# The last two value products of a block move beside the next block's first scores, and the attention steps are spread evenly

## Chip, core and metric

The kernel runs on one core of one Trainium2 chip. The metric is the device time of one execution in microseconds. Three executions of the kernel before took 840.87, 840.63 and 839.79 us, so the median is 840.63 us.

## What is computed

Windowed attention over 8 batches, 8 heads, 576 positions and head dimension 64, and then a feed-forward layer on the 4608 resulting tokens of width 512:

```
scores = q @ k^T / 8, kept where 0 <= row - col < 64
attn   = softmax(scores);  x = attn @ v, heads side by side: 4608 x 512
h = x @ w_in                               (512 x 2048)
g = h where h >= 1, 0 where h <= -1, else (h + 1)^2 / 4
out = g @ w_out                            (2048 x 512)
```

Products of full float32 precision are made of three matmuls each (high by high, high by low, low by high), so every operand is split into a rounded high part and a low rest.

## The kernel before

**Tiles and blocks.** The tokens are cut into nine tiles of 512. The first three (t = 0, 1, 2; `PLAIN = 3`) go through the feed-forward layer chunk by chunk: 16 chunks f, each an in-projection (`ffn_in`, L1153, 12 matmuls into one bank of the PSUM pool `ps_h`), a gate on ScalarE, VectorE and GpSimd (`add_gate`: relu L1163, square L1168, gate L1175, high part L1180, low part L1185), and an out-projection (`ffn_out`, L1199, 12 matmuls into four banks `acc`). The other six tiles are handled in pairs as three blocks (`SUPERS = 3`): sums of weight quarters and of token quarters replace one product in eight, so a block is 56 products into `ps_h` and `acc` (`ffn_product`, L928; I write P) and 56 out of it into `acc` (`out_product`, L1014; O), 6 matmuls each. The weight sums are made while tiles 1 and 2 run (`add_sums`: L842, L849, L857 on VectorE or GpSimd, a copy on ScalarE, a store to `kept` in DRAM), in two buffers, so a half of a sum waits until the store of the half before the last has landed.

**Attention steps.** A step s covers 128 tokens, four to a tile. Its scores (S, `att_scores`, L439) go to two banks `ps_a`; VectorE masks them and takes the maximum (L462, eight instructions and as many reads), ScalarE takes the exponentials (L482), VectorE or GpSimd normalizes (L501), VectorE transposes (L508), and the result goes through DRAM (`moved`, then `ptd`). After that the values (V, `att_values`, L552) can be multiplied. Steps 0 to 11 belong to the three tiles, 12 to 19, 20 to 27 and 28 to 35 to the three blocks; a block takes its steps in the order 0, 4, 1, 5, 2, 6, 3, 7. When the values of a token quarter's two steps are there, VectorE, ScalarE and GpSimd build the token sums and their high and low parts (`add_build`: L587, L290, L623).

**Pairs.** From step 9 on TensorE takes the scores of one step and the values of an earlier one as one piece, without a break (`do` in `add_step`). The values of tile 2's last step and of the last two steps of each block (`BEHIND = 2`) are pieces of their own, and so are the scores of steps 12 and 16, and of the first two steps of the later blocks. A value product alone takes a bank of `ps_a`; a paired one takes a bank of `ps_h` or of `acc` (the name `pj` in `add_step`). `ps_a` and `ps_h` have two banks each, `acc` has four.

**Order.** `Plan` sets the order on every engine in advance: each piece of work has a key (its due time), a cost and its dependences, and each engine takes the piece that could start first, by key among those about equal. Keys of attention steps come from `a_keys`: backwards from the block's start with a lead and a distance (`A_SUPER`), in units of about four microseconds. The instructions then run in that order, engine by engine, whatever the chip's times turn out to be.

Of the kernel before, what the change touches and what calls it, by code (L numbers as in the profile page):

```python
# [22 lines left out]
SB = 2 * QB  # L23
# [5 lines left out]
TILES = [512] * 9  # L29
# [11 lines left out]
JOIN = 8  # L41
BEHIND = 2
E_SPAN = 0.29
E_LEAD = 9.81
W_LEAD = -1.5
W_FIRST = (17.22, -2.0, 1.41, 1.48, -3.05)
W_STEP = 1.02
L_LEAD = -0.77
W_LATE = (3.72, -1.06, -2.67, 7.19, 13.28, 13.03, 18.55)
# [6 lines left out]
M_LATE = 1  # L56
W0_STEP = 12.29
FINE = 4
# [5 lines left out]
A_LEAD = 4.64  # L64
O_LAG = 2.79
O_LAG_DMA = 2300
# [11 lines left out]
B_PE = 2210  # L78
B_DUE = (2.44, -1.28, -0.74)
B_STEP = 5.68  # L80
B_FIRST = 1.45
A_END = 5.86
V_PE = 1270
NORM = dict(Pool=800, DVE=480), dict(DVE=610)
G_LATE = (1.94, 1.65, -4.21, -4.45, 2.08)
D_LATE = (-0.7, 0.46, 6.3, -3.34, 6.37, 0.12)
# [11 lines left out]
SUM_KEEP = 1150  # L98
V_LATE_2 = 14.69
PATIENCE = dict(ACT=300, DVE=0, Pool=303, PE=0, SP=0)  # L100
# [5 lines left out]
SUPERS = 3  # L106
H_STEP = 18.67
S_LATE = 1.62
S_PACE = 2.47
O_CHANGE = 3.33, 3.2, 4.7  # L110
EARLY_2 = 2.71
A_SUPER = ((7.71, 2.68), (9.52, 4.03))
A_ORDER = (0, 4, 1, 5, 2, 6, 3, 7)
BUILD = (-12.04, 16.74)
X_SLOTS = 4, 0, 6, 1, 2, 3
# [3 lines left out]
WRITES = (1, None), (2, 1), (0, None), (3, 2), (3, 3), (1, 2), (2, 2)  # L119
R_LEAD = -4.99  # L120
R_LOAD = 430
L_DVE = 4, 6, 8
G_LEAD = (3.99, -2.67, 0.94, -2.12)
OP_LEAD = 10.45
D_LEAD = 0.72

# [92 lines left out]
def banded_attention_then_ffn(ctx: ExitStack, tc: tile.TileContext, q, k, v, w, masks, out, out_t, dims):  # L219
# [448 lines left out]
    def add_step(t, i):  # L668
# [3 lines left out]
        masked = s < PE_MASKS  # L672
        joined = JOIN <= s and t < PLAIN and i < TILES[t] // SB - 1
        pt, pv = ("ps_h", "acc") if s < LENT else ("ps_a", "ps_a")
# [22 lines left out]
        if before and (t < PLAIN or len(before) == BEHIND):  # L697
            sv = min(before, key=seq.get)
            needs_v, gives_v, split = before.pop(sv)
            pj = "acc" if t > PLAIN and key < block_key((t - PLAIN) // 2 - 1, 1) else "ps_h"  # L700

            def do(e):
                att_scores(s, masked, ps)
                att_values(sv, pj)

            xs = add(
                key, dict(PE=B_PE), do, needs + needs_v, takes=[ps, ps, "sm", pj],
                gives=[("qt", xq), ("kt", xk)] + gives_v,
            )
            split(xs, key, pj)  # L710
        else:
            xs = add(
                key, dict(PE=S_PE[near(s)] + 500 * masked), lambda e: att_scores(s, masked, ps), needs,
                takes=[ps, ps, "sm"], gives=[("qt", xq), ("kt", xk)],
            )
# [79 lines left out]
        if joined or t >= PLAIN:  # L795
            before[s] = needs, gives, split
        if t >= PLAIN and i == A_ORDER[-1]:
            for sw in sorted(before, key=seq.get):
# [186 lines left out]
    def block_key(u, l):  # L985
        return step(PLAIN) + (2 * u + l) * H_STEP

# [294 lines left out]
    def add_ffn(t):  # L1282
        first, before, x_out = {}, [x_in[t - 1]] if t else [], {}
        for f in range(NF):
            for r, key in parts(t, f):
# [9 lines left out]
                for i in subs(r):  # L1295
                    x_in[t, i] = xi
                xa, _, xh, xl = add_gate(t, f, r, key, G_LATE if t == 0 else [0] * 5, [xi], [("ps_h", xi)])
                over = {x_out[i] for i in subs(r)} if f else set()
# [57 lines left out]
    for t in range(PLAIN):  # L1356
        if t + 1 < PLAIN:
            for i in range(TILES[t + 1] // SB):
                add_step(t + 1, i)
        add_ffn(t)  # L1360
        if t == 0:
            for l in range(2):
                for n in range(NF // 2):
                    add_sums(l, n)
    for u in range(SUPERS):
        for i in A_ORDER:
            add_step(PLAIN + 2 * u, i)
        add_super(u)
    with tc.manual_schedule():
# [57 lines left out]
```

## Time and profile before

| | us |
|---|---|
| median of three runs | 840.63 |
| the profiled execution | 843.4 |
| its span, first to last instruction | 841.6 |
| TensorE busy in the span | 821.6 (98%) |
| VectorE / ScalarE / GpSimd busy | 687.0 / 533.5 / 213.8 |

The span is from the first to the last instruction of the core; the execution's own time lies 1.8 us above it. TensorE's granted clock was 0.994 of 2.4 GHz over the span. A matmul's row shows when it starts; the next one can start before it ends, so the distance between starts is what a piece costs.

### The profile page before, as it was taken

The page shows a single profiled execution, that of the slowest core. Times are in us where ns is not written, and L with a number is a line of the kernel's source. Part 1 is how long each engine was busy: PE and PEld are TensorE (multiplying, and loading weights), DVE is VectorE, ACT ScalarE, POOL GpSimd, SP SyncE. Part 2 cuts the span into 40 slices and gives each one's busy share as a digit, 9 for nine tenths or more (in the row PEclk, how much of TensorE's full clock was granted, in tenths as well). Part 3 has the DMA queues.
Part 4 walks back from the last instruction along what each step waited for, and adds up shares of the span by engine and source line. Part 5 has one row for each costly group of instructions (what it writes and reads, how often), then busy time and mean ns, then how long its engine had stood idle before and what let it go on. Part 6 is the DMA issues. An engine that isn't in the chain of part 4 may idle for free.

```text
span 841.6 us, 18582 instructions
## 1 busy us (share of the span) xinstructions
PE 821.6 (98%) x6588; PEld 672.1 (80%) x6588; DVE 687.0 (82%) x1613; ACT 533.5 (63%) x1303; POOL 213.8 (25%) x226
## 2 busy tenths in 40 slices
PE   7889999999999999999999999999999999999998
PEld 5767788878787878788888888888888888888886
DVE  6999996468757789888899986888999848878964
ACT  5999983545654764756775654777756536566442
POOL 1000014335664636221233320122332201100100
PEclk8999999999999999999999999999999999999999
DMA  8994359996788797788898898888888877777775
GB/s 322 394 375 170 100 165 331 362 331 200 214 265 262 219 285 235 271 252 272 272 333 253 284 316 281 269 268 282 302 252 244 294 230 198 192 195 193 198 224 164
DMA packets 151901, 216.08 MB, mean 257 GB/s; under 512 B 11904, under 2 KB 75264, under 8 KB 151808
## 3 DMA queue, kind: packets, MB, share of 16 engines
q1 hardware_dynamic: 151520, 213.97, 80.2%
q8 instruction: 53, 0.87, 0.4%
q10 hardware_dynamic: 288, 0.92, 0.3%
q14 instruction: 40, 0.33, 0.1%
HBM read 163.72 MB, written 51.12 MB: 255 GB/s over the span
## 4 chain that ended last, share of the span: by engine, by line
PE 75%; DVE 10%; DMA 7%; ACT 3%; issue 2%; POOL 2%; SPq 1%; ACTq 0%; POOLq 0%; DVEq 0%
PE acc L1014 27%; PE ps_h L928 14%; PE acc L928 14%; PE ps_h L1153 8%; PE acc L1199 7%; DMA kept<-u 4%; PE ps_a L439 2%; DVE u L842 1%; PE ps_a L552 1%; DVE u L857 1%; PE ps_h L552 1%; DVE u L849 1%; DMA raw<-in_w 1%; DVE wts L358 1%; DMA kt<-in_k 1%
## 5 line engine op out<-in xcount | busy, mean ns | idle before, releaser
L1014 PE MATMUL acc<-op,wts 128*128 128x512 f32 x576 | 137.7, 390 | 0.0
L1153 PE MATMUL ps_h<-xh,wts 128*128 128x512 f32 (+1 forms) x424 | 131.2, 376 | 6.1 <-DVE a L1175 4.4
L290 ACT CAST op<-g 128x512 fp32r<-128x512 f32 x129 | 80.2, 622 | 77.4 <-PE acc L1014 49.3
L1014 PEld LDWEIGHTS acc<-op,wts 128*128 128x128 f32 x576 | 107.8, 188 | 22.5
L1199 PE MATMUL acc<-wts,gh 128*128 128x512 f32 x384 | 120.1, 394 | 0.7 <-ACT gh L1180 0.7
L482 ACT ACTIVATE sm<-sm,nm 128x96 f32<-128x96 f32 x248 | 89.5, 363 | 12.3 <-DVE nm L462 11.6
L1153 PEld LDWEIGHTS ps_h<-xh,wts 128*128 128x128 f32 x424 | 78.0, 190 | 22.6 <-DVE a L1175 6.5
L1005 DVE TENSOR_TENSOR op<-g,op 128x512 fp32r<-128x512 f32 x107 | 76.7, 718 | 20.7 <-ACT op L290 20.2
L928 PE MATMUL ps_h<-wts 128*128 128x512 f32 x360 | 92.0, 391 | 0.0
L928 PE MATMUL acc<-wts 128*128 128x512 f32 x360 | 91.5, 389 | 0.0
L1199 PEld LDWEIGHTS acc<-wts,gh 128*128 128x128 f32 x384 | 70.8, 188 | 16.0 <-ACT gh L1180 1.1
L1168 ACT ACTIVATE a<-a 128x512 f32<-128x512 f32 (+1 forms) x125 | 77.1, 617 | 3.8
L1153 PE MATMUL ps_h<-xl,wts 128*128 128x512 f32 (+1 forms) x212 | 78.8, 372 | 0.6 <-DVE xl L565 0.6
L928 PEld LDWEIGHTS acc<-wts 128*128 128x128 f32 x360 | 67.5, 188 | 14.2
L928 PEld LDWEIGHTS ps_h<-wts 128*128 128x128 f32 x360 | 67.2, 188 | 14.2
L1199 PE MATMUL acc<-wts,gl 128*128 128x512 f32 x192 | 75.3, 392 | 1.4 <-DVE gl L1185 1.4
L1163 ACT ACTIVATE a<-g 128x512 f32<-128x512 f32 x96 | 60.5, 630 | 19.4 <-DVE g L943 14.0
L1175 DVE SCALAR_TENSOR_TENSOR g<-a,g 128x512 f32<-128x512 f32 x96 | 68.1, 716 | 3.8 <-ACT a L1168 3.2
L1005 POOL TENSOR_TENSOR op<-g,op 128x512 fp32r<-128x512 f32 x28 | 36.1, 1295 | 129.5 <-ACT op L290 118.1
L1185 POOL TENSOR_TENSOR gl<-a,gh 128x512 fp32r<-128x512 f32 (+1 forms) x34 | 48.6, 1429 | 45.0 <-ACT gh L1180 43.2
L992 DVE TENSOR_TENSOR g<-g 128x512 f32<-128x512 f32 x83 | 58.4, 717 | 0.5
L1175 DVE SCALAR_TENSOR_TENSOR a<-a,ps_h 128x512 f32<-128x512 f32 (+1 forms) x53 | 33.3, 628 | 25.1 <-ACT a L1168 24.9
(145 smaller groups left out, 1544.5 us busy)
## 6 DMA issues: line engine op xcount, KB each, us to landing
wts<-kept SPq DMA_DIRECT2D x240, 256.0 KB, 3.6
vt<-in_v SPq DMA_DIRECT2D x72, 256.0 KB, 4.9
ptd<-moved SPq DMA_DIRECT2D x31, 512.0 KB, 4.7
kt<-in_k SPq DMA_DIRECT2D x35, 384.0 KB, 5.1
kept<-wts SPq DMA_DIRECT2D x48, 256.0 KB, 4.8
gh<-kept SPq DMA_DIRECT2D x48, 256.0 KB, 3.7
gl<-kept SPq DMA_DIRECT2D x48, 256.0 KB, 3.6
raw<-in_w SPq DMA_DIRECT2D x12, 1023.8 KB, 10.6
```

The source lines that it names most:

```text
L290: nc.scalar.copy(dst, src)
L482: nc.scalar.activation(t, t, AF.Exp, bias=nm[:, g:g + 1], scale=-1.0, accum_out=den[:, g:g + 1])
L928: nc.tensor.matmul(ps, lhsT=r[:, part, cp], rhs=x_op(k, xp)[:, cp], start=j in (0, 1, 3, 4) and i == 0 and cp == 0, stop=j in (1, 2, 5, 6) ...
L992: engine[eng].tensor_tensor(out=g[:, out], in0=g[:, a], in1=g[:, b], op=op)
L1005: engine[eng].tensor_tensor(out=low, in0=g_of(n)[:, of], in1=high.bitcast(F32), op=ALU.subtract)
L1014: nc.tensor.matmul(opened[b][m], lhsT=r[:, part, m], rhs=op[xp], start=j in (0, 1, 3, 4) and i == 0 and n == 0, stop=j in (1, 2, 5, 6) and ...
L1153: nc.tensor.matmul(ps, lhsT=wts[f, 0][:, part, c * P:(c + 1) * P], rhs=x[:, c, r], start=(c == 0 and j == 0), stop=(c == NP - 1 and j == 2),)
L1163: nc.scalar.activation(gs[t, f, r.start][0], phs[t, f, r.start], AF.Relu, bias=0.5, scale=0.5)
L1168: nc.scalar.activation(a, a, AF.Square)
L1175: nc.vector.scalar_tensor_tensor(out=ps if t >= PLAIN else a, in0=a, scalar=1.0, in1=ps, op0=ALU.min, op1=ALU.max)
L1185: engine[eng].tensor_tensor(out=g[2], in0=g[0], in1=g[1].bitcast(F32), op=ALU.subtract)
L1199: nc.tensor.matmul(acc[t, i][:, n], lhsT=g[:, sub], rhs=wts[f, 1][:, part, n], start=(q == 0 and j == 0), stop=(q == NF - 1 and j == 2 and ...
```

## The change

Every step of tile 2 and of the blocks keeps its values for a later step's scores. The first two steps of a block are now planned before the feed-forward work of the tile or block ahead (`add_ffn(2)`, `add_super(u)`), and they take over the last two value products. Only the last block's last two value products stay alone. The bank that a paired value product takes is `ps_h`, except while a block's P run, where it is `acc`. The distance of steps in the later blocks is 4.53 instead of 4.03 units with a lead of 19.01 instead of 9.52. Gates of tiles 1 and 2 get offsets of their own (`G_NEXT`), and some 30 numbers of the planner are others.

```
-W_LEAD = -1.5
+W_LEAD = -1.6
-L_LEAD = -0.77
+L_LEAD = -0.48
...
+G_NEXT = ((4.83, -5.19, 1.49, -0.74, -2.85), (-0.09, 2.02, 1.4, -0.55, 3.26))
...
-S_LATE = 1.62
-S_PACE = 2.47
+S_LATE = 10.09
+S_PACE = 2.87
...
-A_SUPER = ((7.71, 2.68), (9.52, 4.03))
+A_SUPER = ((4.31, 2.6), (19.01, 4.53))
...
-        joined = JOIN <= s and t < PLAIN and i < TILES[t] // SB - 1
+        joined = JOIN <= s and t < PLAIN
...
-            pj = "acc" if t > PLAIN and key < block_key((t - PLAIN) // 2 - 1, 1) else "ps_h"
+            u = (t - PLAIN) // 2 - 1
+            pj = "acc" if u >= 0 and block_key(u, 0) <= key < block_key(u, 1) else "ps_h"
...
-        if t >= PLAIN and i == A_ORDER[-1]:
+        if t == PLAIN + 2 * (SUPERS - 1) and i == A_ORDER[-1]:
...
-                xa, _, xh, xl = add_gate(t, f, r, key, G_LATE if t == 0 else [0] * 5, [xi], [("ps_h", xi)])
+                xa, _, xh, xl = add_gate(t, f, r, key, G_LATE if t == 0 else G_NEXT[t - 1], [xi], [("ps_h", xi)])
...
+        else:
+            for i in A_ORDER[:BEHIND]:
+                add_step(PLAIN, i)
         add_ffn(t)
...
     for u in range(SUPERS):
-        for i in A_ORDER:
+        for i in A_ORDER[BEHIND:]:
             add_step(PLAIN + 2 * u, i)
+        if u + 1 < SUPERS:
+            for i in A_ORDER[:BEHIND]:
+                add_step(PLAIN + 2 * u + 2, i)
         add_super(u)
```

Up to the first pair (scores of step 9 with values of step 8) TensorE's order is the same in both. From there on, three places. In the changed kernel a line's number is one higher from L87 on and two higher from L700 on.

TensorE, the start of block 0. Before, the scores of step 24 stand alone between the last out-projection of tile 2 and the first P:

```order
L1199 MATMUL acc<-wts,gh 128x512 x2
L1199 MATMUL acc<-wts,gl 128x512
L439 MATMUL ps_a<-kt,qt 32x96 x32
L928 MATMUL ps_h<-wts 128x512 x6
L928 MATMUL acc<-wts 128x512 x6
```

Now step 24 is three pieces earlier, and the first scores after the start are those of step 25, with the values of step 24:

```order
L1201 MATMUL acc<-wts,gl 128x512
L930 MATMUL ps_h<-wts 128x512 x6
L930 MATMUL acc<-wts 128x512 x6
L930 MATMUL ps_h<-wts 128x512 x6
L440 MATMUL ps_a<-kt,qt 32x96 x32
L553 MATMUL acc<-ptd,vt 64x64 x16
L930 MATMUL acc<-wts 128x512 x6
```

Over the whole program there were 6 score pieces and 7 value pieces alone from step 12 on, and 21 pairs; now there are 1, 2 and 26.

TensorE, tile 2. Before, the values of step 11 stand alone, in a bank of `ps_a`, inside an out-projection:

```order
L1199 MATMUL acc<-wts,gh 128x512 x2
L1199 MATMUL acc<-wts,gl 128x512
L552 MATMUL ps_a<-ptd,vt 64x64 x16
L1199 MATMUL acc<-wts,gh 128x512 x2
L1199 MATMUL acc<-wts,gl 128x512
```

Now all values of this stretch are paired and take a bank of `ps_h`, which the in-projections use. Here, scores of step 17 with values of step 16, an in-projection stands directly before and directly after:

```order
L1155 MATMUL ps_h<-xl,wts 128x512
L1155 MATMUL ps_h<-xh,wts 128x512
L440 MATMUL ps_a<-kt,qt 32x96 x32
L553 MATMUL ps_h<-ptd,vt 64x64 x16
L1155 MATMUL ps_h<-xh,wts 128x512
L1155 MATMUL ps_h<-xl,wts 128x512
```

Between the first pair and the first P, 9 values went through `ps_h`, and now 13 do.

VectorE, tile 2. Before, this is what stood ahead of the gate of the in-projection before the pair of steps 19 and 18 (from the low part of a weight sum on; L842 is the first row of the next half sum):

```order
L857 TENSOR_TENSOR u<-u,o 128x512 [waits Activation_49]
L493 TENSOR_SCALAR den<-den 128x8
L494 RECIPROCAL den<-den 128x8 [waits DVE_49]
L501 TENSOR_TENSOR sm<-sm,den 128x768 [waits DVE_49]
L842 TENSOR_TENSOR u<-wts 128x2x128 [waits DMAHW4_49,Pool_49]
L508 STREAM_TRANSPOSE sm<-sm 128x768 [waits DVE_49]
L1175 SCALAR_TENSOR_TENSOR a<-a,ps_h 128x512 [waits Activation_49]
```

Now ahead of the gate before the pair of steps 19 and 18:

```order
L509 STREAM_TRANSPOSE sm<-sm 128x768 [waits DVE_49]
L859 TENSOR_TENSOR u<-u,o 128x512 [waits Activation_49]
L844 TENSOR_TENSOR u<-wts 128x2x128 [waits DMAHW4_49]
L588 TENSOR_TENSOR u<-raw 128x256
L1177 SCALAR_TENSOR_TENSOR a<-a,ps_h 128x512 [waits Activation_49]
```

The first row of a half sum, which waits for a store, still stands in front of the gate.

## Rows read from the trace of the kernel before

**Rows 1.** The profile's page, busy time of each engine, its share of the span and its instructions.

```profile
PE 821.6 (98%) x6588; PEld 672.1 (80%) x6588; DVE 687.0 (82%) x1613; ACT 533.5 (63%) x1303; POOL 213.8 (25%) x226
```

**Rows 2.** Busy time by stretch: start and end, length, then for TensorE, its weight loads, VectorE, ScalarE and GpSimd the busy us (instructions), the granted clock, the share of the DMA engines, GB/s.

```profile
0.00:25.00 25.00, 17.81 (x232) 14.32 (x232) 16.37 (x46) 16.47 (x62) 2.91 (x16) 0.86 0.91 332
25.00:50.00 25.00, 22.35 (x210) 19.68 (x211) 23.51 (x58) 23.08 (x55) 0.00 (x0) 0.93 1.00 392
50.00:75.00 25.00, 22.70 (x164) 16.71 (x164) 24.60 (x59) 24.79 (x60) 0.00 (x0) 1.00 0.75 293
...
150.00:200.00 50.00, 49.14 (x389) 39.92 (x388) 32.73 (x87) 28.68 (x73) 19.42 (x20) 1.00 0.96 315
...
250.00:300.00 50.00, 49.23 (x563) 40.09 (x562) 40.45 (x123) 29.73 (x89) 26.30 (x32) 1.00 0.85 256
300.00:346.00 46.00, 43.34 (x428) 34.50 (x431) 39.55 (x115) 27.10 (x80) 24.04 (x22) 1.00 0.77 233
346.00:430.00 84.00, 84.00 (x704) 68.93 (x699) 70.64 (x169) 58.11 (x148) 19.66 (x19) 1.00 0.86 285
430.00:514.00 84.00, 84.00 (x692) 68.86 (x681) 75.58 (x169) 50.42 (x125) 23.60 (x19) 1.00 0.89 289
...
760.00:842.00 82.00, 78.04 (x345) 64.31 (x343) 58.86 (x90) 35.39 (x57) 2.59 (x2) 1.00 0.67 193
```

**Rows 3.** TensorE in order of time, scores alone between two P of block 1: start us, duration, line, shapes, count.

```profile
529.65 1.52 PE L928 MATMUL ps_h<-wts 128*128 128x512 f32 x6
531.10 1.00 PE L439 MATMUL ps_a<-kt,qt 64*32 64x96 f32 x64
532.03 1.66 PE L928 MATMUL acc<-wts 128*128 128x512 f32 x6
533.52 1.54 PE L928 MATMUL ps_h<-wts,gh 128*128 128x512 f32 x6
534.90 1.52 PE L928 MATMUL acc<-wts,gl 128*128 128x512 f32 x6
```

**Rows 4.** TensorE in order of time, values alone between two O of block 0 (the first row is two O).

```profile
498.61 2.88 PE L1014 MATMUL acc<-op,wts 128*128 128x512 f32 x12
501.42 1.15 PE L552 MATMUL ps_a<-ptd,vt 128*64 128x64 f32 x32
502.50 1.66 PE L1014 MATMUL acc<-op,gh 128*128 128x512 f32 x6
504.00 1.52 PE L1014 MATMUL acc<-op,gl 128*128 128x512 f32 x6
505.36 0.39 PE L1014 MATMUL acc<-gh,wts 128*128 128x512 f32 x1
```

**Rows 5.** TensorE in order of time, a pair of scores and values between two P of block 1.

```profile
567.06 1.52 PE L928 MATMUL acc<-wts 128*128 128x512 f32 x6
568.51 1.00 PE L439 MATMUL ps_a<-kt,qt 64*32 64x96 f32 x64
569.44 1.15 PE L552 MATMUL acc<-ptd,vt 128*64 128x64 f32 x32
570.52 1.66 PE L928 MATMUL ps_h<-wts 128*128 128x512 f32 x6
572.01 1.52 PE L928 MATMUL acc<-wts 128*128 128x512 f32 x6
573.37 1.52 PE L928 MATMUL ps_h<-wts 128*128 128x512 f32 x6
```

**Rows 6.** TensorE in order of time, the first matmul of five in-projections that follow a pair in tiles 1 and 2, with the idle time before it and what ended it.

```profile
187.32 0.50 PE L1153 MATMUL ps_h<-xh,wts 128*128 128x512 f32 x1 [0.86 <-DVE a L1175]
...
244.41 0.50 PE L1153 MATMUL ps_h<-xh,wts 128*128 128x512 f32 x1
...
271.05 0.50 PE L1153 MATMUL ps_h<-xh,wts 128*128 128x512 f32 x1 [0.34 <-DVE a L1175]
...
297.80 0.50 PE L1153 MATMUL ps_h<-xh,wts 128*128 128x512 f32 x1 [0.43 <-DVE a L1175]
...
312.86 0.50 PE L1153 MATMUL ps_h<-xh,wts 128*128 128x512 f32 x1 [1.63 <-DVE a L1175]
```

**Rows 7.** ScalarE and VectorE in order of time, relu and gate before the first of these waits.

```profile
185.28 0.59 ACT L1163 ACTIVATE a<-ps_h 128x512 f32<-128x512 f32 x1
...
186.57 0.69 DVE L1175 SCALAR_TENSOR_TENSOR a<-a,ps_h 128x512 f32<-128x512 f32 x1 [0.47 <-ACT a L1168]
```

**Rows 8.** VectorE in order of time before the longest of these waits.

```profile
310.91 0.42 DVE L842 TENSOR_TENSOR u<-wts 128x256 f32<-128x256 f32 x1 [2.59 <-DMA kept<-u]
...
311.26 0.97 DVE L508 STREAM_TRANSPOSE sm<-sm 128x768 f32<-128x768 f32 x1
...
312.15 0.65 DVE L1175 SCALAR_TENSOR_TENSOR a<-a,ps_h 128x512 f32<-128x512 f32 x1
```

**Rows 9.** Who waited for whom on VectorE from 146 to 346 us: total us, times, longest us.

```profile
DVE u L842 <- DMA kept<-u: 15.0, 8, 2.9
```

**Rows 10.** TensorE in order of time, the scores of steps 20 and 24, just before block 0.

```profile
340.19 1.00 PE L439 MATMUL ps_a<-kt,qt 64*32 64x96 f32 x64
...
344.84 0.32 PE L439 MATMUL ps_a<-kt,qt 64*32 64x96 f32 x2 [0.69 <-PE acc L1199]
345.50 0.98 PE L439 MATMUL ps_a<-kt,qt 64*32 64x96 f32 x62 [0.34 <-DVE nm L462]
```

**Rows 11.** VectorE in order of time, the first mask instruction on the scores of step 20.

```profile
343.95 0.24 DVE L462 CUSTOM_DVE_ANT_0 sm<-ps_a,nmsk 128x96 f32<-128x96 f32 x1
```

More of the change, by code (lines that the diff above doesn't have):

```diff
@@ L56 @@
 M_LATE = 1
-W0_STEP = 12.29
+W0_STEP = 12.11
 FINE = 4
@@ L64 @@
 A_LEAD = 4.64
-O_LAG = 2.79
+O_LAG = 2.96
 O_LAG_DMA = 2300
@@ L78 @@
 B_PE = 2210
[L79 to L82, printed above, removed]
+B_DUE = (2.48, -0.99, -1.74)
+B_STEP = 5.64
+B_FIRST = 1.28
+A_END = 4.85
 V_PE = 1270
 NORM = dict(Pool=800, DVE=480), dict(DVE=610)
-G_LATE = (1.94, 1.65, -4.21, -4.45, 2.08)
+G_LATE = (1.94, 1.65, -3.6, -4.45, 2.08)
+G_NEXT = ((4.83, -5.19, 1.49, -0.74, -2.85), (-0.09, 2.02, 1.4, -0.55, 3.26))
 D_LATE = (-0.7, 0.46, 6.3, -3.34, 6.37, 0.12)
@@ L98 @@
 SUM_KEEP = 1150
-V_LATE_2 = 14.69
+V_LATE_2 = 15.15
 PATIENCE = dict(ACT=300, DVE=0, Pool=303, PE=0, SP=0)
@@ L106 @@
 SUPERS = 3
-H_STEP = 18.67
-S_LATE = 1.62
-S_PACE = 2.47
+H_STEP = 18.91
+S_LATE = 10.09
+S_PACE = 2.87
 O_CHANGE = 3.33, 3.2, 4.7
-EARLY_2 = 2.71
-A_SUPER = ((7.71, 2.68), (9.52, 4.03))
+EARLY_2 = 5.18
+A_SUPER = ((4.31, 2.6), (19.01, 4.53))
 A_ORDER = (0, 4, 1, 5, 2, 6, 3, 7)
-BUILD = (-12.04, 16.74)
+BUILD = (-0.78, 33.82)
 X_SLOTS = 4, 0, 6, 1, 2, 3
@@ L119 @@
 WRITES = (1, None), (2, 1), (0, None), (3, 2), (3, 3), (1, 2), (2, 2)
-R_LEAD = -4.99
+R_LEAD = 1.64
 R_LOAD = 430
 L_DVE = 4, 6, 8
-G_LEAD = (3.99, -2.67, 0.94, -2.12)
-OP_LEAD = 10.45
-D_LEAD = 0.72
+G_LEAD = (5.41, -1.42, 0.45, -3.54)
+OP_LEAD = 12.27
+D_LEAD = 3.15
 class Plan:
```

## The prediction

> **What bounds the kernel now.** Start with the engines' busy times [rows 1]: TensorE is busy 821.6 of 841.6 us, so 20.0 us of idle time are all that better waiting could give back; everything else has to come from shorter TensorE work. Then see by stretch where the 20 us lie [rows 2]. The first 75 us hold 7.19 + 2.65 + 2.30 = 12.1 us, the last stretch 3.96 us (its tail is the final outputs and their stores). In the blocks, from 346 us on, TensorE is busy without a gap, 84.00 of 84 us twice. The rest lies in tiles 1 and 2: 0.86 us in 150 to 200, 0.77 in 250 to 300, 2.66 in 300 to 346.
>
> The order of time names these 4.3 us. Four in-projections wait for a gate, 0.86 + 0.34 + 0.43 + 1.63 = 3.26 us [rows 6], and the scores of step 24 wait 0.69 + 0.34 = 1.03 us [rows 10]. Each of the four is the first in-projection after a pair whose values took a bank of `ps_h`. With two banks, the in-projection then needs the bank of the in-projection just before the pair, and gets it when that one's gate is done. The gate is late because VectorE runs in order: before the longest wait it stood 2.59 us at the first row of a half sum, until a store to `kept` had landed, and the gate was two rows behind [rows 8]. In tiles 1 and 2 VectorE waits 15.0 us in 8 such places [rows 9], and most of these happen to cost TensorE nothing.
>
> **The change part by part.**
>
> *Up to 150 us: nothing.* TensorE's order is the same up to the pair of steps 9 and 8, and so are the rows of VectorE and ScalarE that belong to it. The 12.1 us at the start stay.
>
> *Five more pairs.* A product of 6 matmuls takes 573.37 - 572.01 = 1.36 us between starts [rows 5]. Scores alone: 534.90 - 529.65 = 5.25 us for three products, less 4.08, leaves 1.17 us [rows 3]. Values alone: 505.36 - 498.61 = 6.75 us for four products, less 5.44, leaves 1.31 us [rows 4]. A pair: 573.37 - 567.06 = 6.31 us, less 4.08, leaves 2.23 us [rows 5]. So a pair costs 0.25 us less than its halves apart: one change between kinds of matmul falls away. The counts of the order (6, 7 and 21 pieces before; 1, 2 and 26 now) give five such savings, 1.25 us, all on TensorE and so on the path. Bounds: none, if the saving is an artefact of where I measured, and twice that, 2.5 us, which is more than the differing first products of these rows allow.
>
> *Steps 20 and 24.* They stood 4.65 us apart, between the end of tile 2 and block 0. Step 20's scores began at 340.19, but VectorE came to mask them only at 343.95 [rows 11], since building tokens and sums was ahead in its queue; two banks of `ps_a` were thus taken until 345.5 [rows 10]. Now steps lie evenly: from step 12 on at least 36 matmuls (36 x 1.36 / 6 = 8.2 us) and a pair lie between two starts of scores. The 1.03 us go. What would be late next there is the token build of block 0's last quarter. From its values to the first P it had 24 matmuls, two score pieces and the wait, 5.4 + 2.3 + 1.0 = 8.7 us, and was in time; now it has 72 matmuls and a pair, 18.5 us. Bounds 0 to 1.03; I take 1.03.
>
> *Values through `ps_h` in tiles 1 and 2.* This speaks against the change. Values 11, 15 and 19 leave `ps_a`, value 20 comes in, and all take `ps_h`: 13 instead of 9. What counts is how long the gate has. Where one out-projection and the pair stand between two in-projections, it has 2 x 1.36 + 2.23 = 4.95 us. Such places were 7, and the four waits are at four of them; now they are 8. At one more place, steps 17 and 16, there is only the pair, 2.2 us, while relu, square and gate took 187.32 - 185.28 = 2.04 us from the relu's start to TensorE's with VectorE free [rows 6, 7]. There the two gates stand back to back on ScalarE and VectorE, so it may just fit; I count 0.15 us. At 4 of the 7 places a half sum's waiting row stood ahead of the gate on VectorE, and these cost 0.34 + 0.43 + 1.63 + 0 = 2.4 us, 0.6 each; the other three cost 0.86, 0.3 each. Now such a row is ahead of 7 of the 8: 7 x 0.6 + 0.3 + 0.15 = 4.65 us if each costs what it did. Against that the sums get later keys and a wider pace (2.87 instead of 2.47 units). A half sum's turn lasts (346 - 150) / 32 = 6 us, and 16% of it is 1 us; VectorE's mean wait for a store was 15.0 / 8 = 1.9 us [rows 9], so it would about halve, and the sum is 7 x 0.3 + 0.45 = 2.55 us. I take the middle, 3.6 us, 0.3 more than now. Bounds: all waits gone, -3.26, and doubled, +3.26.
>
> *The blocks.* Four pairs lie in P now instead of three, and O loses one. VectorE was the fullest in O, 75.58 of 84 us [rows 2], without one wait of TensorE; P had 70.64. Between the first and last addition of P the order now has 170 VectorE rows in block 0 (148 before) and 167 in block 1 (164), and 189 as before in O of block 0. The 16 mask rows of one more step are most of the difference. P of block 0 thus rises by about 5 us of VectorE work, to where O was. I cost it at nothing; its cover is that 8 us of every 84 are still free, and if it fails, additions of P get late and each costs TensorE up to the 0.7 us of one VectorE row. Loads and stores have other places on SyncE's queue too; the blocks showed no gap [rows 2], so no transfer was late there, and nothing is taken for that.
>
> *Sum.* -1.25 - 1.03 + 0.3 = -1.98 us. Against the profiled execution, 843.4 us, that gives 841.4; that execution lies 2.8 us above the median of the three runs, and I carry the difference to the median: 840.63 - 1.98 = **838.7 us**, 0.24% faster. About 0.2%, or 1.7 us, is what a measurement can tell from no change.
>
> **The rivals.**
>
> *One bubble for each value through `ps_h`.* The four waits over nine values are 0.36 us a value [rows 6]; thirteen values make 4.7 us, 1.45 more than before: 840.63 - 2.28 + 1.45 = 839.8 us, no change. For it: every wait after 75 us but step 24's follows such a value. Against it: 244.41 is such a place too and shows none [rows 6], and the short places grow from 7 to 9 and not from 9 to 13.
> The Trainium skill, page Perfetto Trace Analysis, section Optimization Strategy, has a rule for this: the same gap repeating on the engine that should be saturated can mean that there are too few buffers for the next tile. By that rule more users of two banks bring more gaps, and this rival's 839.8 us rather than 838.7; that the waits here all follow a value in a two-bank pool agrees with it, the free place at 244.41 does not.
>
> *The gates get free.* Sums with later keys and wider pace stop holding VectorE before a gate. All 3.26 us go, and the time is 840.63 - 2.28 - 3.26 = 835.1 us. For it: the 1.63 and 0.34 us waits have a waiting half sum directly ahead [rows 8]. Against it: such rows now stand ahead of more of these gates.
>
> *The gates become the bound (slower).* At the nine short places of tiles 1 and 2 every in-projection waits as long as the longest did, 1.63 us [rows 6]: 14.7 us, 11.4 more than before, 840.63 - 2.28 + 11.4 = 849.8 us. It is slower by over 0.2% from a mean of (3.26 + 2.28 + 1.7) / 9 = 0.80 us a place. For it: gates of 2 us in places of 2.1 and 4.95 us, and a store that holds VectorE up to 2.9 us [rows 9]. Against it: the mean of the seven places was 0.47 us.
>
> *The pairs bring nothing.* The order has the pairs, but the 0.25 us come back as longer neighbours, as the 1.66 us of the first product after each kind of piece could suggest [rows 3 to 5]. Then only step 24's wait goes: 840.63 - 1.03 + 0.3 = 839.9 us, no change. Against it: the three prices were taken over the neighbours.
>
> **How the numbers follow.** My forecast has 0.45; since 838.7 lies 0.3 us from the 0.2% line, at 838.95, I give 0.14 of it to no change. Free gates have 0.20, one bubble per value 0.18, pairs that bring nothing 0.05, and gates as the bound 0.12, of which 0.02 stays under the 0.80 us. Faster: 0.31 + 0.20 = 0.51. The same: 0.14 + 0.18 + 0.05 + 0.02 = 0.39. Slower: 0.10. The range goes from free gates, 835.1, to doubled gate waits, 840.63 - 2.28 + 3.26 = 841.6; what is left out is the most of the slower case and a little below free gates.
>
> **What would show it.** Right: 26 pairs of 2.23 us each and only one score piece and two value pieces alone after step 9; no wait of TensorE at scores just before block 0; none in the blocks; in-projections after pairs waiting 2 to 5 us in all, each ended by L1177. Wrong: waits of more than 7 us there; a wait at scores, an addition or a build in P; or the first P of block 0 earlier by less than the pairs and step 24 give. Before, it stood 0.93 us after the scores of step 24 [rows 3, 10], at 346.4. Three pairs and step 24's wait take 1.8 us off, the moved pair of steps 21 and 20 adds 2.2 ahead of it, and the gates add 0.3: it must stand near 347.1 us.

## The result and the profile after

The changed kernel takes 846.10 us (median of 845.06, 845.71, 846.49 and 847.50), beside 840.21 us for the kernel before; the ratio is 1.0071, 95% interval [1.0053, 1.0088]. Run again beside others it was 1.0056 [1.0043, 1.0069]. So it is slower by 0.6 to 0.7%, where 0.24% faster was forecast. The profiled execution took 845.06 us.

Busy time of the engines, from the page of the changed kernel, as in [rows 1]:

```profile
PE 819.7 (97%) x6588; PEld 668.1 (79%) x6588; DVE 692.8 (82%) x1625; ACT 535.6 (64%) x1308; POOL 200.5 (24%) x209
```

By stretch, columns as in [rows 2]:

```profile
0.00:25.00 25.00, 16.45 (x238) 12.95 (x239) 17.92 (x51) 18.38 (x71) 2.93 (x16) 1.00 0.95 342
25.00:50.00 25.00, 22.87 (x276) 19.13 (x275) 24.31 (x58) 23.59 (x51) 0.00 (x0) 1.00 1.02 415
...
300.00:346.00 46.00, 45.10 (x544) 36.39 (x543) 42.30 (x133) 30.02 (x98) 25.13 (x25) 1.00 0.81 254
346.00:430.00 84.00, 80.59 (x697) 64.99 (x696) 73.14 (x177) 59.12 (x150) 14.07 (x12) 1.00 0.93 308
430.00:514.00 84.00, 84.00 (x716) 68.89 (x715) 81.24 (x193) 53.94 (x141) 28.99 (x25) 1.00 0.85 274
```

TensorE is busy 1.9 us less than in [rows 1], and yet the kernel is slower. The first 84 us of the blocks, which had no gap before, have 84 - 80.59 = 3.41 us now. TensorE in order of time names them, and the waits in tile 2:

```profile
190.27 0.50 PE L1155 MATMUL ps_h<-xh,wts 128*128 128x512 f32 x1 [0.36 <-DVE a L1177]
204.94 0.98 PE L440 MATMUL ps_a<-kt,qt 64*32 64x96 f32 x62 [0.94 <-DVE nm L463]
...
263.91 0.50 PE L1201 MATMUL acc<-wts,gl 128*128 128x512 f32 x1 [0.62 <-POOL gl L1187]
...
327.22 0.50 PE L1155 MATMUL ps_h<-xh,wts 128*128 128x512 f32 x1 [0.90 <-DVE a L1177]
...
345.95 0.61 PE L930 MATMUL ps_h<-wts 128*128 128x512 f32 x2
348.29 1.21 PE L930 MATMUL ps_h<-wts 128*128 128x512 f32 x4 [1.73 <-DVE wts L624]
...
365.20 1.62 PE L930 MATMUL ps_h<-wts 128*128 128x512 f32 x6 [1.16 <-DMA wts<-kept]
367.35 1.62 PE L930 MATMUL acc<-wts 128*128 128x512 f32 x6 [0.53 <-DMA wts<-kept]
```

The very first product of block 0 stops after two matmuls for a row of the token build (L624), and two products 19 and 21 us after it wait for their weights.

**Where the time went.** The profiled execution of the kernel before, 843.4 us, lay above its median. A second one (the run before_again below) took 839.57 us and is the one to compare with. The start of the 241st in-projection matmul (134.16 us before, 133.82 after) is a common mark; from there the table has the distances to the first P and between the first P and the first O of each block, from TensorE's rows (P of block 0 in the changed kernel: 437.66 - 345.95). "Due" is the difference that the prices of the prediction give for the pieces in the stretch (pair 2.23, scores alone 1.17, values alone 1.31 us).

| stretch | before | changed | again | due | excess |
|---|---|---|---|---|---|
| mark to first P | 208.37 | 212.13 | 210.49 | +1.48 | 2.28, again 0.64 |
| P of block 0 | 85.14 | 91.71 | 92.73 | +2.23 | **4.34, again 5.36** |
| O of block 0 | 84.53 | 83.16 | 83.16 | -1.56 | 0.19 |
| P of block 1 | 86.15 | 87.35 | 87.35 | +1.06 | 0.14 |
| O of block 1 | 83.37 | 78.95 | 78.95 | -4.46 | 0.04 |

Due is -1.25 us in all, the five more pairs. The excess is 6.99 us, so the changed kernel should lie 5.74 us behind, and the two executions differ by 845.06 - 839.57 = 5.49. Most of the loss stands in P of block 0. The stretch up to the first P is the uncertain one: the first execution of the kernel before took 209.87 us there, 1.5 us more than the second, while its P of block 0 took 85.09.

### The profile page after: what moved, and what is told of

It reads as the page before. It is cut to its first block, busy times and chain, and to the rows that moved or that the text cites. A ratio compares the mean times of both kernels' runs of the same rounds, so it can differ in the third digit from the quotient of the medians.

```text
span 843.2 us, 18581 instructions
## 1 busy us (share of the span) xinstructions
PE 819.7 (97%) x6588; PEld 668.1 (79%) x6588; DVE 692.8 (82%) x1625; ACT 535.6 (64%) x1308; POOL 200.5 (24%) x209
## 4 chain that ended last, share of the span: by engine, by line
PE 77%; DVE 9%; DMA 8%; ACT 2%; issue 2%; POOL 1%; SPq 1%; DVEq 0%; ACTq 0%; POOLq 0%
PE acc L1016 27%; PE acc L930 13%; PE ps_h L930 13%; PE ps_h L1155 9%; PE acc L1201 8%; PE ps_a L440 2%; DMA kept<-u 2%; DMA raw<-in_w 2%; DVE u L851 1%; PE acc L553 1%; DMA wts<-kept 1%; DMA vt<-in_v 1%; PE ps_h L553 1%; DVE a L1177 1%; DMA kt<-in_k 1%
## 5 line engine op out<-in xcount | busy, mean ns | idle before, releaser
L291 ACT CAST op<-g 128x512 fp32r<-128x512 f32 x124 | 77.3, 623 | 81.9 <-PE acc L1016 45.2
L1007 DVE TENSOR_TENSOR op<-g,op 128x512 fp32r<-128x512 f32 x120 | 86.8, 728 | 19.3 <-ACT op L291 18.5
L1201 PEld LDWEIGHTS acc<-wts,gh 128*128 128x128 f32 x384 | 70.7, 188 | 16.8 <-ACT gh L1182 1.9
L1187 POOL TENSOR_TENSOR gl<-a,gh 128x512 fp32r<-128x512 f32 (+1 forms) x34 | 45.1, 1327 | 43.0 <-ACT gh L1182 40.1
L945 DVE TENSOR_TENSOR g<-g,acc 128x512 f32<-128x512 f32 x60 | 41.1, 685 | 15.2 <-PE acc L930 10.1
L945 DVE TENSOR_TENSOR g<-g,ps_h 128x512 f32<-128x512 f32 x60 | 41.0, 683 | 13.2 <-PE ps_h L930 12.9
```

What stands on the lines that cost most here:

```text
L291: nc.scalar.copy(dst, src)
L945: nc.vector.tensor_tensor(out=g[:, to], in0=g[:, of], in1=prods[u, n, b], op=ALU.add)
L1007: engine[eng].tensor_tensor(out=low, in0=g_of(n)[:, of], in1=high.bitcast(F32), op=ALU.subtract)
L1201: nc.tensor.matmul(acc[t, i][:, n], lhsT=g[:, sub], rhs=wts[f, 1][:, part, n], start=(q == 0 and j == 0), stop=(q == NF - 1 and j == 2 and ...
```

## Experiments

Two theories. **A**: the weight sums end inside block 0 now (last stores at 358 and 368 us, before at 338), and their VectorE rows and stores hold up build and weight loads. **B**: the attention steps themselves do it, which are now dense around the start of block 0, with their masks, transposes, hops through DRAM and loads.

### The two kernels again

No edit. 

> The changed kernel once more, with a second profile. If the three stalls at the start of block 0 (1.73, 1.16 and 0.53 us in the first profile) belong to the order of the instructions, they stand at the same three products again, each within 0.5 us, and the time is 845 to 847 us. If they are luck of the transfers, the two that wait for a load change by over 1 us, and the time with them.

845.12 us, ratio 1.0056. The first stall is 1.73 us again, the two later ones stand at the same products:

```profile
365.19 1.62 PE L930 MATMUL ps_h<-wts 128*128 128x512 f32 x6 [1.46 <-DVE g L1177]
368.15 1.63 PE L930 MATMUL acc<-wts 128*128 128x512 f32 x6 [1.33 <-DMA wts<-kept]
```

The first of these rows names VectorE, but the load of this product's weights (issued at 358.14 us) landed 0.13 us before it starts, as in the first profile, so I count it as a load. The places belong to the order. The sizes of the two on loads vary: 2.79 us together instead of 1.69, and the last one is 0.80 us longer, more than the 0.5 us of the expectation.

> The kernel before once more, for a second profile: its first profiled execution lay 2.8 us above the median. If that was the start alone (granted clock 0.86 and 0.93 in the first 50 us), TensorE's waits in tiles 1 and 2 are 4.3 us again and the same in place. If the waits vary from execution to execution, the gates wait 1 us or more less in all, and part of what the changed kernel was to gain there was never in the median.

840.48 us, ratio 1.0003 [0.9991, 1.0015]. TensorE's waits from 146 to 346 us in this execution (total us, times, longest):

```profile
PE ps_h L1153 <- DVE a L1175: 1.1, 2, 0.8
PE ps_a L439 <- PE acc L1199: 0.7, 1, 0.7
PE ps_h L552 <- DVE u L849: 0.6, 1, 0.6
PE ps_a L439 <- DVE nm L462: 0.3, 1, 0.3
```

Step 24's wait is the same 0.7 + 0.3 us; the gates cost 1.1 us instead of 3.26 [rows 6]. One value waits too, for 0.6 us, which did not show in the first execution. Both guesses hold a part: the clock in the first 50 us was 0.93 and 1.00 instead of 0.86 and 0.93, and the waits vary too. In this execution, 0.9 us under the median of its run, two thirds of the 3.26 us are not there.

### Structure and numbers apart

Structure alone: the changed code with

```
G_NEXT = ((0,) * 5, (0,) * 5)
S_LATE, S_PACE, A_SUPER, BUILD, ... as before
```

> The joins, the order of planning and the choice of bank alone: all of the planner's numbers are those of the kernel before, the new gate offsets zero. Theories A and B both blame numbers: no stall above 0.5 us in the first 25 us of block 0, and five more pairs (1.25 us) and step 24's wait (1.03 us) gained, less what the gates cost: 838.5 to 840.5 us. Theory C (the joined pieces themselves cost, by the banks that they hold): 842 us or more, with waits of in-projections or of the first products of a block that end on VectorE.

864.47 us, ratio 1.0289 [1.0274, 1.0305]. A and B did not say this. C had a time of 842 us or more, but its waits were to end on VectorE, and the two longest, 7.31 and 7.27 us, end on ScalarE's part of a token build and on a hop. Steps keep their old distance, so the values of step 19 come with the scores of step 24, just ahead of block 0, and those of step 28 with the scores of step 29, right behind step 32's. TensorE in order of time:

```profile
349.73 1.22 PE L930 MATMUL ps_h<-wts 128*128 128x512 f32 x2 [7.31 <-ACT wts L291]
352.49 2.08 PE L930 MATMUL ps_h<-wts 128*128 128x512 f32 x4 [1.54 <-POOL wts L624]
...
536.78 1.44 PE L553 MATMUL acc<-ptd,vt 128*64 128x64 f32 x22 [7.27 <-DMA ptd<-moved]
```

A joined value waits for the next step's scores; the build of the block needs that value, and the block's first product needs the build. So the join forces two more steps to an early place, and the change needs the new lead and distance of steps to give it.

Numbers alone: the kernel before with all new constants but the gate offsets. 

> The kernel before, its pieces alone as they were, with all of the planner's new numbers (but the gate offsets, which it has no place for). With the run that had the structure alone this makes a table of two by two. If the numbers bring the loss whatever the structure, block 0 stalls over 3 us at its start and the time is 844 to 847 us, and the structure then brings its 1.25 us of pairs on top. If numbers and structure only fit together, it is worse than the changed kernel, 847 us or more.

847.56 us (842.93 to 848.48; two of the six executions took 843), ratio 1.0071 [1.0047, 1.0096]. Block 0 stalls 1.94 and 1.35 us on weight loads and 1.78 on a hop. The numbers bring a loss without the joins too; with them alone the block is as bad as in the changed kernel. The time lies in the range of the second guess, but its ratio is that of the changed kernel, so it does not show that numbers and structure only fit together.

### The sums (theory A)

```
S_LATE, S_PACE = 1.62, 2.47     # sums_old, in the changed kernel
S_LATE, S_PACE = 10.09, 2.87    # before_sums, in the kernel before
S_LATE = 1.62                   # late_old, in the changed kernel
S_LATE, S_PACE = 1.62, 2.7      # sums_27, in the changed kernel
```

> The changed kernel with the old lateness and pace of the weight sums (1.62 and 2.47). Theory A (late sums: the last half sums now end inside P of block 0, where their VectorE rows hold the token build and their stores hold the weight loads): the 3.4 us of stalls in the first 25 us of block 0 fall under 0.5 us, and the time is 846.1 - 3.4 = 842.7 us, within 1 us. Theory B (the steps, now dense around the start of block 0, with their loads, hops and builds, do it): the stalls stay above 2 us and the time stays at 845 us or more.

846.08 us (841.86 to 849.72), ratio 1.0064. A is right on the place: the last stores are issued at 344 and 345 us, block 0 has no stall, and its P takes 85.12 us, what its pieces are due. (Step 25's pair stands ahead of the first P in this order.) But the time does not fall. VectorE waits 16.8 us for stores in tiles 1 and 2, once 7.3 us (11.4 and 4.5 in the changed kernel), step 11's hop is late, and its values, now joined with the scores of step 16, hold TensorE:

```profile
176.38 1.15 PE L553 MATMUL ps_h<-ptd,vt 128*64 128x64 f32 x32 [3.59 <-DMA ptd<-moved]
```

The hop is not late because of VectorE's waits: its transposing starts 0.3 us later than in the changed kernel, its read is issued 1.0 us later and lands 2.1 us later (176.25 and 174.18 us). The delay arises on SyncE's queue and on the way.

> The kernel before with the new lateness and pace of the sums (10.09 and 2.87) and nothing else. Theory A: TensorE stalls 2 to 3.5 us in the first 25 us of block 0, and the time is 842.2 to 843.7 us. Theory B: no stall above 0.5 us there, and the time is within 1 us of 840.2.

842.70 us, ratio 1.0032 [1.0019, 1.0045], with one stall of 2.50 us, 12 us into block 0. As A had it: late sums cost the kernel before 2.5 us in block 0. The row of this wait names ScalarE; but the load `gh<-kept`, issued 8.0 us after the first P, right behind four stores of sums, landed 0.13 us before the product starts, so it is a load as well.

> The changed kernel with the old lateness of the sums (1.62 instead of 10.09) and their new pace; TensorE's order stays the same up to the first pair in block 0. Theory A, as it stands after the first runs (the end of the sums makes the stalls at the start of block 0, their pace makes VectorE's waits for stores in tiles 1 and 2): no stall over 0.5 us in the first 25 us of block 0, waits in tiles 1 and 2 of 2.4 to 3.4 us as in the changed kernel, so 845.5 - 3.9 = 841.6 us, within 1.2. Theory B (the steps' own loads and builds stall block 0): stalls of 2 us or more there, 844 us or more.

846.38 us, ratio 1.0070. The edit did less than meant: at the new pace the last store came at 362.7 instead of 368.7 us, still in block 0. The stalls there were 1.01, 0.74 and 0.74 us, and a gate waited 1.95 us in tile 2. It does not test A as it was meant to, and tells nothing between A and B.

> The changed kernel with the old lateness (1.62) and a pace of the sums between the two (2.7): the last store stands ahead of block 0's loads on SyncE's queue again, and VectorE should wait less for stores than at the old pace (16.8 us there). Theory A: no stall over 0.5 us at the start of block 0; if the wait for the hop of step 11 (3.59 us at the old pace) is gone too, 840 to 842 us, the best of both; if it stays, 844 to 846 us.

851.07 us, ratio 1.0123. Wrong: step 11's wait stayed (3.63 us), and the build came 2.33 and 2.27 us late. Step 25 stood ahead of the first P in this order. One stall on a load, 1.20 us, was left 17 us into block 0, though the last store had landed at the first P: a late store is not needed for it.

### The build's due time, the loads' lead, and plain traffic

```
BUILD = (-12.04, 16.74)         # build_old, in the changed kernel
R_LEAD = -4.99                  # ring_old, in the changed kernel
# traffic, in the kernel before, in ring_load:
if (l, u) == (0, 0) and n < 2 and 1 < j < 4:
    nc.sync.dma_start(out=spare, in_=kept[0][0][:, 0])
```

> The changed kernel with the old due times of the token build. If the first stall of block 0 (1.73 us, on L624) comes from the later due time of the last quarter's build, it is gone here, the two stalls on weight loads stay at 1.7 to 2.8 us together, and the time is 845.5 - 1.7 = 843.8 us. If the build is late because of the rows of sums and masks ahead of it on VectorE, the stall stays over 1 us and the time at 845 to 846 us.

846.91 us, ratio 1.0081. The stall on L624 is gone, but step 25 moved ahead of the first P, a product behind it waited 3.06 us (for ScalarE, L291), and the loads 1.39 and 1.51. The due time only moves the place.

> The changed kernel with the old lead of the weight loads in the blocks (-4.99 instead of 1.64); TensorE's order is the same throughout. If the two stalls on weight loads in block 0 come from their place on SyncE's queue, behind stores and the steps' loads, they change by over 1 us together, to the better or the worse. If they come from transfers that share full DMA engines (share 0.97 to 1.07 from 348 to 372 us), they stay within 0.7 us of 1.7 to 2.8, and the time at 844.5 to 846.5 us.

844.49 us, ratio 1.0058. Stalls 1.73, 1.32 and 0.52 us, P of block 0 91.77 us. The edit did nothing: all 742 transfers, and the instructions of every engine, stand in the same order as in the changed kernel. So this is a third execution of the same program, and whether the lead of the loads matters was not tested.

> The kernel before, with four copies of 256 KB from DRAM to DRAM behind four of the first weight loads of block 0 (1 MB read and 1 MB written, nobody waits for them). If full DMA engines are what the weight loads of block 0 suffer from, TensorE stalls 1 us or more on loads in the first 30 us of block 0, where it has no stall now, and the time is 841.3 to 843.5 us. If the loads there have room, no stall over 0.3 us and 840.3 us, within 0.8.

842.00 us, ratio 1.0016 [1.0004, 1.0029], and no stall in the blocks. Three of the four copies ran between 2 us ahead of the first P and 10 us behind it (the fourth 47 us ahead), with the DMA engines at a share of 0.95 to 1.04. So full DMA engines alone didn't stop TensorE there. The loads that stop the changed kernel are issued later, from 12 us on; their stage was not tested. Of the small loss, 0.45 us stand in P of block 0 (85.58 us), without a wait that the profile shows.

### Half by half at the start of block 0

The first two runs leave out the last weight sum: its stores (no_stores), or stores and rows (no_sums). Its place in DRAM is filled with plain weights by four other stores, the filler.

```
 def sum_keep(l, n, c):
+    if (l, n) == (1, 7): return      # no_sums: in sum_whole, sum_sums, sum_high, sum_low too
```

> The changed kernel, in which the last weight sum (both its halves) is still computed but not stored in block 0; its place in DRAM is filled before, around 230 to 280 us, with plain weights (so the outputs that use this sum are not the reference's). If the 1 MB that these stores put into the first 25 us of block 0 makes the two stalls on weight loads, they fall under 0.7 us together (1.7 to 2.8 before), the first stall on L624 stays at 1.7, and the time falls to 843 to 844 us. If the sum's rows on VectorE or the steps make them, they stay and the time stays at 845 us or more.

> As the run before, and the last weight sum's rows on VectorE, GpSimd and ScalarE left out too. Theory A whole (late sums, rows and stores): the first stall falls under 1 us as well, no stall on loads over 0.5 us is left, 841.5 to 843 us. Theory B (masks, hops, loads and builds of the steps alone fill VectorE and the transfers): first stall 1.4 us or more, and at least 1 us on loads; 844 us or more.

847.10 us (1.0082) and 847.36 (1.0092). Both have a side effect: the filler stood on SyncE's queue at 156 to 172 us, and step 11's values waited 3.00 and 3.36 us. In block 0, stalls of 1.72 and 1.26 us, and of 1.19 and 1.09. So without the stores one of the two stalls on loads is gone (1.26 us are left of 1.69 to 2.79 together), and without the rows a third of the first stall. The next runs are without the side effect:

```
 # no_sums2: filler beside the stores of sums (1, 1) and (1, 2)
 # no_hops:
+LIGHT = 24, 21, 25
-... lambda e, j=j: att_write(s, j) ...      -... lambda e: att_read() ...
+... s in LIGHT or att_write(s, j) ...       +... s in LIGHT or att_read() ...
 # light: att_normalize and att_turn in the same way; light_no_sums: light and no_sums2
```

> The changed kernel without the last weight sum (rows and stores of both halves), as in the run no_sums; its place in DRAM is now filled with plain weights beside the stores of two sums before it, so that nothing new is on SyncE's queue while step 11's hop goes through (outputs that use this sum are not the reference's). The first half of block 0 took 91.7 and 92.7 us in the changed kernel; the 85.1 of the kernel before plus its one pair more would be 87.3, so 4.4 to 5.4 us are to be explained. Theory A (late sums alone): under 88.5 us. Theory A and B together, each about half: 89.5 to 90.5, with a first stall of about 1.2 us, and 843 to 844.5 us in all. Theory B alone: over 91 us.

> The changed kernel in which the probabilities of steps 24, 21 and 25 don't make their way through DRAM (three times two writes of 192 KB and a read of 512 KB less around the start of block 0; their values are computed with what an earlier step left, so the output is not the reference's). If these transfers, in packets under 2 KB, are what the weight loads of block 0 stand behind, the stalls on loads (1.2 to 1.5 and 0.5 to 1.3 us) fall under 0.7 us together; the first stall, on the build, stays at 1.7. If not, the first half of block 0 stays at 91.5 us or more.

> As no_hops, and steps 24, 21 and 25 are not normalized or transposed either (two VectorE rows each, 1.9 us a step). If VectorE's rows of the steps make the first stall, it falls from 1.73 to under 1 us, and with the loads' stalls gone too the first half of block 0 takes 88 to 90 us and the whole 842 to 843.5 us. If the sums' rows make it, the first stall stays over 1.4.

> Both: no last weight sum, and no hop, no normalizing and no transposing for steps 24, 21 and 25. If sums and steps together are all that fills the start of block 0, its first half takes 87.3 to 88.5 us with no stall over 0.5 us, and the whole 841 to 842.5 us. If a third thing is in it (the order of the build's own rows, or the place of the weight loads), 2 us of stalls are left.

| | us | ratio | P of block 0 | first stall | on loads |
|---|---|---|---|---|---|
| changed | 846.10 | 1.0071 [1.0053, 1.0088] | 91.71 | 1.73 | 1.16 + 0.53 |
| changed, again | 845.12 | 1.0056 [1.0043, 1.0069] | 92.73 | 1.73 | 1.46 + 1.33 |
| changed, third (ring_old) | 844.49 | 1.0058 [1.0041, 1.0074] | 91.77 | 1.73 | 1.32 + 0.52 |
| no_sums2 | 843.02 | 1.0048 [1.0032, 1.0064] | 90.39 | 0.50 | 1.90 |
| no_hops | 841.87 | 1.0031 [1.0021, 1.0041] | 89.34 | 1.84 | 0 |
| light | 840.98 | 1.0024 [1.0015, 1.0033] | 88.38 | 0.89 | 0 |
| light_no_sums | 841.25 | 1.0026 [1.0016, 1.0037] | 87.93 | 0.42 | 0 |

TensorE's waits in the first half of block 0, from the wait views of no_sums2, of no_hops, of light and of light_no_sums (total us, times, longest; line numbers differ between the runs):

```profile
PE ps_h L944 <- DMA wts<-kept: 1.9, 1, 1.9
PE ps_h L944 <- DVE wts L624: 0.5, 1, 0.5
```

```profile
PE ps_h L931 <- DVE wts L625: 1.8, 1, 1.8
```

```profile
PE ps_h L931 <- DVE wts L625: 0.9, 1, 0.9
```

```profile
PE ps_h L945 <- DVE wts L625: 0.4, 1, 0.4
```

This tells the parts apart. The stalls on loads need the steps' hops: without three hops both are gone, sums or not, and without the last sum 1.90 us are left. But hops alone do not make them at every place: sums_old had all hops, no late sum and no stall on a load. The first stall is VectorE's queue, with a share of 1.73 - 0.50 = 1.23 us that goes with the sum's rows and one of 1.84 - 0.89 = 0.95 us with the two rows a step; the shares overlap, as either alone leaves less than the other took. With both out, the half block takes 87.93 us, 0.56 over the 87.37 that its pieces are due. A and B both have a part, and B has the larger: P takes 2.4 to 3.4 us less than in the three executions of the changed kernel without the hops (89.34 us), and 1.3 to 2.3 us less without the sum (90.39), one execution each. In the whole time only the runs without hops lie clear of the changed kernel, no_hops just so; the interval of no_sums2 overlaps with those of the changed kernel.

This is not the whole loss. light and light_no_sums still lie 0.24 and 0.26% (2.0 and 2.2 us) behind the kernel before, while their five pairs should have put them 1.25 us ahead. Their later half blocks are within 0.03 us of what is due, and their P of block 0 explains 1.0 and 0.6 us; the other 2 to 3 us must lie ahead of the first P and stay open.

My reason for the hops, small packets, is not borne out: from 346 to 372 us packets under 2 KB were 2555 and 2347 in the two profiles of the changed kernel, 2593 without hops and 1278 without the sum. What changes is the time from issue to landing of the weight loads in that stretch; of before, of the changed kernel and of no_hops:

```profile
DMA to landing us min/median/max: 2.9/4.0/5.6
```

```profile
DMA to landing us min/median/max: 4.9/5.4/7.2
```

```profile
DMA to landing us min/median/max: 2.9/4.8/6.1
```

Both SyncE's queue and the way have a part. The weight load that the first of the stalled products waits for is issued 11.9 us after the first P in the changed kernel and lands 7.2 us later; without hops, 10.0 us after it and 5.0 us later. So 1.9 us come from turns on SyncE's queue (the two writes of a hop take 1.3 us) and 2.2 us from the way; what makes the way longer was not told apart.

### Joins at the later transition alone

The kernel before; block 2's first two scores take block 1's last two values.

```
-A_SUPER = ((7.71, 2.68), (9.52, 4.03))
+A_SUPER = ((7.71, 2.68), (9.52, 4.03), (16, 3.2))
...
-        for i in A_ORDER:
+        for i in A_ORDER[BEHIND if u > 1 else 0:]:
             add_step(PLAIN + 2 * u, i)
+        if u == 1:
+            for i in A_ORDER[:BEHIND]:
+                add_step(PLAIN + 4, i)
```

> The kernel before with the joins at the later transition alone: values of block 1's last two steps with scores of block 2's first two (lead and distance 16 and 3.2 for block 2's steps); all other numbers, tile 2 and the first half of block 0 are those of the kernel before. If the loss of the change sits at the start of block 0 alone, block 0's first half takes 85.1 us as before, no stall over 1 us stands in the later blocks, and two pairs more bring 0.5 us: 839 to 840.3 us, no difference that can be measured. If joins between blocks cost by themselves (banks, hops that are late for the next values), 842 us or more, with stalls at the first pairs of block 1.

849.28 us, ratio 1.0117 [1.0102, 1.0132]. P of block 0 takes 85.09 us, as before, but block 1's first product waits 4.68 and 1.53 us for its token build: the values of step 27 stand right ahead of it. TensorE in order of time, and two stretches (columns as in [rows 2]; the granted clock is the third number from the end):

```profile
519.05 1.22 PE L929 MATMUL ps_h<-wts 128*128 128x512 f32 x2 [4.68 <-ACT wts L290]
521.81 2.07 PE L929 MATMUL ps_h<-wts 128*128 128x512 f32 x4 [1.53 <-POOL wts L623]
523.68 2.76 PE L929 MATMUL acc<-wts 128*128 128x512 f32 x6
```

```profile
517.00:523.00 6.00, 2.41 (x5) 1.50 (x6) 3.43 (x6) 2.62 (x11) 5.41 (x7) 0.50 1.03 369
523.00:529.00 6.00, 6.00 (x20) 4.77 (x19) 0.69 (x1) 1.17 (x2) 0.13 (x1) 0.67 0.70 190
```

So a join is not free at the later place either, when the steps keep a late place; with the distances of the change it is (excess 0.04 to 0.19 us there). No version tried beats the kernel before.

## Why the prediction was wrong

- **Up to 150 us: nothing.** Right. The marks at 134 us (136.55 and 134.16 us before; 133.82 and, in the run again, 135.18 changed) differ as much between executions of one kernel as between the two. The granted clock of the first 25 us, in the same order 0.86, 0.93, 1.00 and 0.86, goes with a part of it.
- **Five more pairs, -1.25 us.** Right. With the prices of [rows 3 to 5] the three later half blocks come out within 0.19 us.
- **Step 24's wait, -1.03 us.** It is gone, and both executions of before had it. But scores of step 12 now wait 0.94 us (0.87 again) for masks, as VectorE stood at a half sum's first row:

```profile
200.03 0.94 DVE L844 TENSOR_TENSOR u<-wts 128x256 f32<-128x256 f32 x2 [2.34 <-DMA kept<-u]
```

The wait was turned into one 140 us earlier, and the step gained about 0.1 us.
- **The token build "now has 72 matmuls and a pair, 18.5 us", and is in time.** Wrong: it is 1.73 us late. I counted TensorE's distance and not VectorE's queue. Before, VectorE's part of the last quarter's build ran almost in one piece, and GpSimd made five of its six low parts (342.07 to 346.67 us):

```profile
340.09 1.46 DVE L587 TENSOR_TENSOR u<-raw 128x256 f32<-128x256 f32 x2 [1.23 <-ACT raw L290]
341.47 0.87 DVE L587 TENSOR_TENSOR u<-raw,u 128x256 f32<-128x256 f32 x2
342.26 1.17 DVE L292 CAST wts<-u 128x512 fp32r<-128x512 f32 x2
343.35 0.68 DVE L623 TENSOR_TENSOR wts<-u,wts 128x512 fp32r<-128x512 f32 x1
```

Now it is spread over 12 us, between half sums, a gate and the masks of step 21:

```profile
336.31 1.52 DVE L588 TENSOR_TENSOR u<-raw 128x256 f32<-128x256 f32 x1
...
340.10 1.36 DVE L851 TENSOR_TENSOR u<-u 128x128 f32<-128x128 f32 x1
342.20 1.12 DVE L859 TENSOR_TENSOR u<-u,o 128x512 fp32r<-128x512 f32 x1 [0.73 <-ACT o L291]
343.24 0.24 DVE L463 CUSTOM_DVE_ANT_0 sm<-ps_a,nmsk 128x96 f32<-128x96 f32 x1
...
344.66 0.68 DVE L624 TENSOR_TENSOR wts<-u,wts 128x512 fp32r<-128x512 f32 x1
...
347.45 0.78 DVE L624 TENSOR_TENSOR wts<-raw,wts 128x256 fp32r<-128x256 f32 x1
```

VectorE makes all six low parts, and its first row comes 8 us after ScalarE has copied the values (336.3 and 328.4 us; before, 340.09 and 340.06). So the plan has a part too, by its new due time and its choice of engine: with the old due time (build_old) this stall is gone, and others take its place.

- **Values through `ps_h`, +0.3 us.** The gates waited 1.45 us in the changed kernel and 0.19 again, not 3.6; more values through `ps_h` did no harm. But the 3.26 us of before were 1.1 in the second execution (1.7 with the value that waits), so there was little to win, and the rival of free gates, near to what again shows, wins nothing. The rival of one bubble a value falls with it: thirteen values had three such waits in one execution and one in the other, nine had four and two. The rule of the Trainium skill (Perfetto Trace Analysis, Optimization Strategy), that a repeated gap can mean too few buffers, is not borne out here. New waits stand at out-projections (0.37 and 0.62 us, again 0.73 and 0.62), one for a low part on GpSimd. The other excess up to the first P, 0.9 to 1.5 us, shows no wait and stays open.
- **The blocks, "I cost it at nothing".** This is the step that failed: 4.3 to 5.4 us in P of block 0. Its cover, "8 us of every 84 are still free", looks at how full VectorE is. But VectorE was no fuller where the loss is: in the first 25 us of block 0 it is busy 22.0 us, and before 22.2 us, without a stall. What counts here is which rows stand ahead of the one that TensorE needs. "The blocks showed no gap, so no transfer was late there, and nothing is taken for that" fails too: the loads had been in time by an unknown margin, and with three hops fewer they are in time again. I had seen sums with later keys and priced them for gates only, not for the block into which they now run.
- **The rivals.** The slower one had 849.8 us by gates; the sign came, the mechanism did not.

## What to carry to other kernels

When a change only moves work to a denser place, look at the first microseconds of the stage that it crowds, queue by queue and row by row in their order, and not at how busy an engine is over the stage; a stage without a gap tells nothing of its slack. A work item that is joined to a later one delays whoever needs its result: follow that result to its first user, along each engine's queue. Take a second execution before counting a wait as something to win. And before reading a run of one changed number, see whether the order of instructions changed at all.

## What was not expected of the hardware

Some long waits of TensorE were followed by a lower granted clock. After the 4.68 us wait of later_joins it was 0.50 (the level of 1.2 GHz) and 0.67 over 12 us, and 6 matmuls took 2.76 us instead of 1.52; after structure's 7.31 us it was 0.50 over six us, after before_sums' 2.50 us 0.82 over eight. After the 1.73 and 1.16 us waits of the changed kernel, after 3.00 us in no_stores and after 3.06 us in build_old, it stayed at 1.00; after 3.59 us at the same place in sums_old it was 0.72 and 0.85. In later_joins the two stretches around this wait are 9.6 us over what their pieces are due (O of block 0 and P of block 1 took 89.84 and 92.15 us, due 85.20 and 87.21), of which the waits are 6.2; the slower matmuls can account for the rest.
